# Filtering the last two column groups by token phase on three engines, with one PSUM pool for two stages

## The chip, the cores and the metric

The kernel runs on one core of a Trainium2 chip. The metric is the device time of one execution in microseconds. The engines are named as the profile names them: PE is TensorE (PEld its weight loads), DVE is VectorE, ACT is ScalarE, POOL is GpSimd, and SP issues most DMAs. Each works through its own instructions in order and waits on semaphores for the others.

## What is computed

An input x of 2048 tokens by 640 features is normalised, filtered in the frequency domain, added to itself, and then goes through a gated block without a nonlinearity:

```python
def _A_ref(x, w_r, w_i):
    X = jnp.fft.rfft2(x, axes=(-2, -1))
    X = X * (w_r + 1j * w_i)
    return jnp.fft.irfft2(X, s=(S, D), axes=(-2, -1))
def _B_ref(x, w_gate, w_up, w_down):
    return ((x @ w_gate) * (x @ w_up)) @ w_down
h = x + _A_ref(layernorm(x), w_r, w_i)
h2 = h + _B_ref(layernorm(h), w_gate, w_up, w_down)
```

S is 2048, D is 640, the real transform has 321 columns, and the inner width of the gated block is 1728.

## The kernel before

The transform over tokens is split as 16 times 128, so a two-dimensional transform, the filter and its inverse become four stages of matrix products.

**Stage one** (lines 200 to 296) runs over 16 tiles t of 128 tokens. `s1_mm(t)` multiplies the folded and normalised tile into two PSUM tiles: `pm` (tag `u`, two buffers) and a remainder `pr` (tag `im2` or `ir2`, one buffer each). Then `s1_main` (L225, ACT) copies `pm` into `s1`, in two halves for the last tile; `s1_hi` (L220, ACT) and `s1_lo` (L229, DVE) write the remainder into `s1r` as a rounded part and its rest. PSUM has eight banks of 512 float32 per partition; `banks("a", name)` closes the pool of PSUM tiles in use and opens another, and stage one works in a pool of its own (`pone`).

**Stage two** (lines 297 to 438) opens the pool `ptwo` and runs over 16 groups g of columns. For each group:

- `d_mm(g)` (L82) multiplies `s1` (eight passes, the main part) and then `s1r` (six products, the remainder) into `re` and `im`; `d_out(g)` copies both to `t` in four ACT instructions (L329 to L332).
- `s2_mm(g)` (L341) multiplies `t` into `u`, a tile of two banks with one buffer, one bank for each half h of the token phases; for the last group it takes `re` and `im` in place of `u`.
- `filt(g)` multiplies by the complex filter. Real and imaginary parts lie on partitions 0 to 63 and 64 to 127, so the crossed product moves between the halves. For most groups DVE does it all, for both h at once: L349 (direct product), L350 and L351 (crossed products), L352 (their sum). For group 15 ACT first copies the crossed parts out of PSUM (L356, L357), DVE makes the direct products (L360), POOL (L366) and DVE (L367) multiply the crossed ones, and DVE adds (L369).
- `is2_mm(g)` (L382, L384, L385) multiplies the filtered `y` into `pm` and `pr`. For group 14 these are buffers of `re` and `im`, for all others `im2` and `ir2`, which have one buffer each, so that group 15 can only start when group 13 has been read out. Row 64 of `pr` is called the edge here.
- `is2_out(g)` copies out: ACT the rounded remainder (L395, the hi copy) and the edge (L396), DVE the rest of the remainder (L397), ACT the main part into `qm` (L398), and POOL two small instructions on the edge row (L400, L401).

The order is written out by hand: the loop at L410 sets, for each g, s2_mm(g), d_mm(g+2), is2_mm(g-1), filt(g), the loads of group g+3, d_out(g+2), is2_out(g-1). At g = 14 both last s2_mm come first, and filt(15) comes between filt(14) and is2_out(13). After the loop follow is2_mm and is2_out of groups 14 and 15. The framework adds the waits: reads of one PSUM bank by different engines are put in program order, and a new pool's tiles wait for the old pool's.

**Stage three** opens two new pools (`py` and `pthree`). `id_mm(t)` (L82, tile `eo`) multiplies `qm` (eight passes) and then the remainder `qr` (five products), `unfold(t)` (L474 to L482) and `is1_mm(t)` make the tokens again. Every id_mm needs all 16 groups, so stage three begins when group 15 has been copied out. The gated block follows; it takes the rest of the time.

Of the kernel before, what the change touches and what calls it, by code (L numbers as in the profile page):

```python
# [46 lines left out]
def tile_spectral_glu(ctx: ExitStack, tc: tile.TileContext, x, wf, wgu, wlast, wdown, wdlast,  # L47
# [12 lines left out]
    def banks(key, name):  # L60
        if key in pools:
            open_pools[key].close()
        open_pools[key] = ExitStack()
        pools[key] = open_pools[key].enter_context(tc.tile_pool(name=name, bufs=2, space=bass.MemoryType.PSUM))

    def bank(tag, bufs=2):
        return pools["a"].tile([P, 512], F32, tag=tag, name=tag, bufs=bufs)
# [7 lines left out]
    def wk(shape, name):  # L75
        return work.tile(shape, F32, tag="wk", name=name)
# [121 lines left out]
    PS1, CR = {}, {}  # L198

    def s1_mm(t):  # L200
        pm, pr = PS1[t] = bank("u"), bank("ir2" if t % 2 else "im2", 1)
        (f, j), c = folded(t), CR[t]
        sums = [(f[:, o:o + P], f[:, o + n:o + n + P]) for o, n in ((31, 160), (353, 161))]
        for k, ls in enumerate((*sums, (view(j, 128, [[2, P]]),), (view(j, 129, [[2, P]]),))):
            for n, l in enumerate(ls):
                nc.tensor.matmul(pm[:, k * P:(k + 1) * P], l, c, start=n == 0, stop=n == len(ls) - 1)  # L206
        nc.tensor.matmul(pr[:, 0:P], j[:, 0:P], c, start=True, stop=True)
# [86 lines left out]
    s1_hi(NT - 1)  # L294
    s1_lo(NT - 1)

    banks("a", "ptwo")
    WM, WI = {}, {}

    def load_wm(g):  # L300
# [33 lines left out]
    def s2_mm(g):  # L334
        if g == NG - 1:
            ps = PU[g] = bank("re"), bank("im")
        else:
            PU[g] = pools["a"].tile([P, 2, 512], F32, tag="u", name="u", bufs=1)
            ps = PU[g][:, 0], PU[g][:, 1]
        for h in range(2):  # L340
            nc.tensor.matmul(ps[h][:, 0:NQ], WM[g][0][:, h], T[g][:, h], start=True, stop=True)  # L341

    def filt(g):
        ps, w = PU[g], WM[g][1]
        y = Y[g] = wk([P, 2, NQ], "y")
        us = wk([P, 2, NQ], "us")
        if g < NG - 1:
            v = ps[:, :, 0:NQ]
            tt(y, v, w[:, 0], op=OP.mult)  # L349
            nc.vector.scalar_tensor_tensor(us[0:64], v[64:128], -1.0, w[64:128, 1], op0=OP.mult, op1=OP.mult)  # L350
            tt(us[64:128], v[0:64], w[0:64, 1], op=OP.mult)  # L351
            tt(y, y, us, op=OP.add)  # L352
            return

        def swap(h):
            act(us[0:64, h], ps[h][64:128, 0:NQ], AF.Copy, scale=-1.0)  # L356
            act(us[64:128, h], ps[h][0:64, 0:NQ], AF.Copy)  # L357

        def direct(h):
            tt(y[:, h], ps[h][:, 0:NQ], w[:, 0, h], op=OP.mult)  # L360

        swap(0)
        direct(1)
        swap(1)
        direct(0)
        nc.gpsimd.tensor_tensor(us[:, 0], us[:, 0], w[:, 1, 0], op=OP.mult)  # L366
        tt(us[:, 1], us[:, 1], w[:, 1, 1], op=OP.mult)  # L367
        for h in (1, 0):
            tt(y[:, h], y[:, h], us[:, h], op=OP.add)  # L369

    def is2_mm(g):
        if g == NG - 2:
            pm, pr = bank("re"), bank("im")
        else:
            pm, pr = bank("im2", 1), bank("ir2", 1)
        PI[g] = pm, pr

        def o(ps, n, c, h):
            return ps[0:n, c * 256:(c + 1) * 256].rearrange("p (a m) -> p a m", m=8)[:, :, 4 * h:4 * h + 4]

        for h in range(2):
            nc.tensor.matmul(o(pr, 65, 0, h), Y[g][:, h, 128:193], inv(g, h), start=True, stop=True)  # L382
        for h in range(2):
            nc.tensor.matmul(o(pm, P, 0, h), Y[g][:, h, 0:128], inv(g, h), start=True, stop=True)  # L384
            nc.tensor.matmul(o(pm, P, 1, h), Y[g][:, h, 193:321], inv(g, h), start=True, stop=True)  # L385

    def inv(g, h):
        return WI[g][:, h].rearrange("p (a m) -> p a m", m=4)

    def is2_out(g):  # L390
        pm, pr = PI[g]
        f = edge[g % 4][0:1]
        r = pr[:, 0:256].rearrange("p (r n m) -> p r n m", r=2, n=NT)
        hi, lo = (qr[n:n + 64, :, :, 8 * g:8 * g + 8] for n in (0, 64))
        act(hi, r[0:64], AF.Copy)  # L395
        act(f, pr[64:65, 0:128], AF.Copy)  # L396
        tt(lo, r[0:64], f32(hi), op=OP.subtract)  # L397
        act(qm[:, :, :, 8 * g:8 * g + 8], pm.rearrange("p (c n m) -> p c n m", c=4, n=NT), AF.Copy)  # L398
        fv = f.rearrange("p (n m) -> p n m", n=NT)
        nc.gpsimd.tensor_copy(hi[0:1, 1], fv)  # L400
        nc.gpsimd.tensor_tensor(lo[0:1, 1], fv, f32(hi[0:1, 1]), op=OP.subtract)  # L401
# [8 lines left out]
    for g in range(NG - 1):  # L410
# [8 lines left out]
            s2_mm(g + 1)  # L419
        if g >= 1:  # L420
            is2_mm(g - 1)
        filt(g)
        if g + 3 < NG:
            load_wm(g + 3)
        if g + 2 < NG:
            d_out(g + 2)
        if g == NG - 2:
            filt(g + 1)
        if g >= 1:
            is2_out(g - 1)  # L430
            if g + 2 < NG:
# [1 line left out]
        if g == 6:  # L433
            nc.sync.dma_start(cit, ci)
            nc.sync.dma_start(imt, imain)
    for g in (NG - 2, NG - 1):
        is2_mm(g)
        is2_out(g)
# [592 lines left out]
```

## Time and profile before

| what | value |
|---|---|
| median of 3 runs | 729.96 us (729.23 to 730.31) |
| the profiled execution | 729.67 us |
| its span | 727.6 us |
| stage two, from d_mm(0) to id_mm(0) | 49.81 to 126.60 us |
| PE busy | 703.7 us (97%) |
| DVE, ACT, POOL busy | 465.5, 251.7, 298.5 us |

The execution's time exceeds its span by 2.1 us, which lie outside the profile. A row of the timeline has the start in us from the span's start, the duration in us, the engine, the line, the operation, what it writes and reads, how many instructions are merged into it, and in brackets how long the engine had been idle and which instruction ended that. A row of the windows has the stretch, then for PE, PEld, DVE, ACT and POOL the busy time and number of instructions, then the granted TensorE clock as a share of full speed, the DMA share and GB/s. A row of the chain has start, duration, engine, tile and line. A float32 product runs as two passes and is counted twice.

### The profile page before, as it was taken

How to read it: one execution, taken by the hardware profiler on the slowest of the kernel's cores; microseconds unless marked ns; L12 is line 12 of the kernel's file. 1: busy time of each engine (PE TensorE's matmuls, PEld its weight loads, DVE VectorE, ACT ScalarE, POOL GpSimd, SP SyncE). 2: the span in 40 equal slices, each digit the busy share in tenths (PEclk: the TensorE clock that was granted, in tenths of full speed). 3: DMA queues.
4: the chain of work that ended last, by engine and by line, in shares of the span. 5: the costliest groups of instructions: out<-in, count | busy, mean ns of one | idle time of the engine just before them, and what ended most of it. 6: DMA issues, size and time to landing. Idle time of an engine off the chain costs nothing.

```text
span 727.6 us, 10120 instructions
## 1 busy us (share of the span) xinstructions
PE 703.7 (97%) x3892; PEld 623.6 (86%) x3892; DVE 465.5 (64%) x802; ACT 251.7 (35%) x480; POOL 298.5 (41%) x274
## 2 busy tenths in 40 slices
PE   7899997999979999999999999999999999999998
PEld 7788997987868898989898888888898989898987
DVE  7967887797766665665555557565555555555554
ACT  4756666355442212222222246332222122222200
POOL 3300113332363554646463633145545546464600
PEclk9999999999989999999999999999999999999999
DMA  9404665000221211101021212311212111010203
GB/s 338 163 1 160 226 219 180 1 1 0 73 73 36 73 37 68 41 25 67 20 72 37 91 62 90 112 65 37 72 37 74 37 71 38 25 66 19 73 1 145
DMA packets 20928, 55.06 MB, mean 76 GB/s; under 512 B 2320, under 2 KB 6928, under 8 KB 20880
## 3 DMA queue, kind: packets, MB, share of 16 engines
q1 hardware_dynamic: 20304, 52.70, 20.7%
q0 software_dynamic: 288, 1.48, 0.6%
q8 instruction: 31, 0.51, 0.3%
q10 hardware_dynamic: 288, 0.23, 0.1%
q14 instruction: 17, 0.14, 0.1%
HBM read 49.16 MB, written 5.24 MB: 75 GB/s over the span
## 4 chain that ended last, share of the span: by engine, by line
PE 83%; DVE 12%; ACT 2%; issue 2%; DMA 1%; POOL 0%; DVEq 0%; ACTq 0%
PE e L82 44%; PE y L82 26%; PE re L82 2%; PE u L341 2%; PE im L82 2%; PE eo L82 2%; DVE fold L190 1%; DVE fold L195 1%; PE ir L382 1%; PE im L385 1%; DVE x L493 1%; PE im L384 1%; DVE bt L560 1%; ACT zt L510 1%; DVE bits L214 1%
## 5 line engine op out<-in xcount | busy, mean ns | idle before, releaser
L82 PE MATMUL e<-xt,wst 128*128 128x512 f32 x864 | 206.8, 390 | 0.0
L82 PE MATMUL y<-wd,ht 128*128 128x320 f32 x1312 | 201.4, 310 | 1.2 <-DVE x L493 1.1
L82 PEld LDWEIGHTS y<-wd,ht 128*128 128x128 f32 x1312 | 195.3, 188 | 5.7 <-DVE x L493 2.7
L82 PEld LDWEIGHTS e<-xt,wst 128*128 128x128 f32 x864 | 160.7, 188 | 31.7
L493 DVE TENSOR_TENSOR x<-y,x 128x640 f32<-128x640 f32 x119 | 97.7, 822 | 73.8 <-PE y L82 73.5
L688 POOL TENSOR_TENSOR wst<-raw,wst 128x1024 fp32r<-128x1024 f32 x24 | 57.9, 2411 | 169.5 <-ACT wst L687 169.5
L699 POOL TENSOR_TENSOR wst<-raw,wst 128x896 fp32r<-128x896 f32 (+1 forms) x48 | 67.8, 1436 | 27.8 <-ACT wst L697 27.8
L82 PE MATMUL e<-t,wst 128*128 128x512 f32 x288 | 74.8, 395 | 4.1 <-ACT wst L697 2.7
L82 PEld LDWEIGHTS e<-t,wst 128*128 128x128 f32 x288 | 54.7, 191 | 16.6 <-ACT wst L697 3.1
L794 ACT ACTIVATE ht<-e 128x512 fp32r<-128x512 f32 x24 | 14.4, 599 | 154.3 <-DVE e L793 154.3
L449 POOL TENSOR_TENSOR wd<-draw,wd 128x640 fp32r<-128x640 f32 x28 | 44.4, 1606 | 47.7 <-ACT wd L448 47.7
L807 ACT ACTIVATE ht<-e 128x512 fp32r<-128x512 f32 x24 | 14.4, 599 | 114.0 <-DVE e L806 114.0
L82 PE MATMUL e<-xt,wdir 128*128 128x512 f32 x180 | 41.9, 392 | 1.1 <-DVE q L479 1.1
L82 PEld LDWEIGHTS e<-xt,wdir 128*128 128x128 f32 x180 | 33.4, 188 | 8.3 <-ACT xt L532 1.3
L82 PE MATMUL e<-ht,wst 128*128 128x512 f32 x144 | 37.8, 399 | 0.0
L206 PE MATMUL u<-bits,fold 128*128 128x128 f32 x192 | 31.9, 310 | 5.9 <-DVE bits L214 2.2
L687 ACT ACTIVATE wst<-raw 128x1024 fp32r<-128x1024 f32 x24 | 25.4, 1060 | 33.4 <-DMA raw<-in_wgu_dram 33.4
L787 DVE TENSOR_TENSOR u<-e,u 128x512 f32<-128x512 f32 x24 | 16.6, 692 | 30.9 <-PE e L82 30.9
L206 PEld LDWEIGHTS u<-bits,fold 128*128 128x128 f32 x192 | 26.8, 209 | 10.1 <-POOL fold L180 4.1
L400 POOL CAST qr<-bits 1x128 fp32r<-1x128 f32 x16 | 4.5, 282 | 71.0 <-DVE qr L397 71.0
L82 PEld LDWEIGHTS e<-ht,wst 128*128 128x128 f32 x144 | 27.9, 194 | 6.0
L781 DVE TENSOR_TENSOR u<-e,p 128x512 f32<-128x512 f32 x24 | 16.6, 692 | 24.0 <-PE e L82 23.0
(178 smaller groups left out, 1042.0 us busy)
## 6 DMA issues: line engine op xcount, KB each, us to landing
raw<-in_wgu_dram SPq DMA_DIRECT2D x24, 640.0 KB, 3.9
wts<-in_wf_dram SPq DMA_DIRECT2D x16, 644.0 KB, 3.9
draw<-in_wdown_dram SPq DMA_DIRECT2D x24, 320.0 KB, 4.3
x<-in_x_dram SPq DMA_DIRECT2D x16, 320.5 KB, 6.4
out_dram<-x SPq DMA_DIRECT2D x15, 320.0 KB, 2.2
bits<-in_mm_dram SPq DMA_DIRECT2D x32, 128.0 KB, 3.8
raw<-in_wgu_dram SPq DMA_DIRECT2D x4, 320.0 KB, 4.2
draw<-in_wdlast_dram SPq DMA_DIRECT2D x4, 320.0 KB, 2.8
```

Source lines behind the costliest of these rows:

```text
L82: nc.tensor.matmul(o, l, r, start=start, stop=stop, skip_group_check=True)
L206: nc.tensor.matmul(pm[:, k * P:(k + 1) * P], l, c, start=n == 0, stop=n == len(ls) - 1)
L341: nc.tensor.matmul(ps[h][:, 0:NQ], WM[g][0][:, h], T[g][:, h], start=True, stop=True)
L449: los.append(lambda r=r, a=a, b=b: engine.tensor_tensor(w[:, 1, a:b], r, f32(w[:, 0, a:b]), op=OP.subtract))
L493: tt(xv, ps[:, :, 0:320], xv, op=OP.add)
L687: act(wa[:, 0], stage[:, 0:1024], AF.Copy)
L688: ptt(wa[:, 1], stage[:, 0:1024], f32(wa[:, 0]), op=OP.subtract)
L699: ptt(ws[:, 1, o:o + b - a], stage[:, a:b], f32(ws[:, 0, o:o + b - a]), op=OP.subtract)
L781: tt(u2, o6, p1, op=OP.add)
L787: tt(u2, o5, u2, op=OP.add)
L794: act(hh[1], o3, AF.Copy)
L807: act(hh[0], o4, AF.Copy)
```

## The change

Stage one takes its `pm` from the tag `im`, and the pool is no longer closed between stages one and two, so that one pool of eight banks serves both. In the filter, groups 14 and 15 are taken by phases (h = 0 and 1). Group 14 phase 0 is done on DVE alone. For the other three, ACT copies the crossed parts out of PSUM, POOL multiplies them, and DVE makes the direct product and the sum. DVE's share of group 15 phase 1 comes behind is2_out(13). `is2_mm` of the two groups takes the products phase by phase, and `is2_out(15)` makes the main copy first.

```diff
@@ -198,7 +198,7 @@
     PS1, CR = {}, {}
 
     def s1_mm(t):
-        pm, pr = PS1[t] = bank("u"), bank("ir2" if t % 2 else "im2", 1)
+        pm, pr = PS1[t] = bank("im"), bank("ir2" if t % 2 else "im2", 1)
         (f, j), c = folded(t), CR[t]
         sums = [(f[:, o:o + P], f[:, o + n:o + n + P]) for o, n in ((31, 160), (353, 161))]
         for k, ls in enumerate((*sums, (view(j, 128, [[2, P]]),), (view(j, 129, [[2, P]]),))):
@@ -294,7 +294,6 @@
     s1_hi(NT - 1)
     s1_lo(NT - 1)
 
-    banks("a", "ptwo")
     WM, WI = {}, {}
 
     def load_wm(g):
@@ -337,36 +336,37 @@
         else:
             PU[g] = pools["a"].tile([P, 2, 512], F32, tag="u", name="u", bufs=1)
             ps = PU[g][:, 0], PU[g][:, 1]
+            if g == NG - 2:
+                PU[g] = ps
         for h in range(2):
             nc.tensor.matmul(ps[h][:, 0:NQ], WM[g][0][:, h], T[g][:, h], start=True, stop=True)
 
     def filt(g):
-        ps, w = PU[g], WM[g][1]
+        v, w = PU[g][:, :, 0:NQ], WM[g][1]
         y = Y[g] = wk([P, 2, NQ], "y")
         us = wk([P, 2, NQ], "us")
-        if g < NG - 1:
-            v = ps[:, :, 0:NQ]
-            tt(y, v, w[:, 0], op=OP.mult)
-            nc.vector.scalar_tensor_tensor(us[0:64], v[64:128], -1.0, w[64:128, 1], op0=OP.mult, op1=OP.mult)
-            tt(us[64:128], v[0:64], w[0:64, 1], op=OP.mult)
-            tt(y, y, us, op=OP.add)
+        tt(y, v, w[:, 0], op=OP.mult)
+        nc.vector.scalar_tensor_tensor(us[0:64], v[64:128], -1.0, w[64:128, 1], op0=OP.mult, op1=OP.mult)
+        tt(us[64:128], v[0:64], w[0:64, 1], op=OP.mult)
+        tt(y, y, us, op=OP.add)
+
+    def filt_half(g, h, alone=False):
+        if h == 0:
+            Y[g] = wk([P, 2, NQ], "y"), wk([P, 2, NQ], "us")
+        y, us = (a[:, h] for a in Y[g])
+        v, w = PU[g][h][:, 0:NQ], WM[g][1]
+        direct = lambda: tt(y, v, w[:, 0, h], op=OP.mult)
+        join = lambda: tt(y, y, us, op=OP.add)
+        if alone:
+            direct()
+            nc.vector.scalar_tensor_tensor(us[0:64], v[64:128], -1.0, w[64:128, 1, h], op0=OP.mult, op1=OP.mult)
+            tt(us[64:128], v[0:64], w[0:64, 1, h], op=OP.mult)
+            join()
             return
-
-        def swap(h):
-            act(us[0:64, h], ps[h][64:128, 0:NQ], AF.Copy, scale=-1.0)
-            act(us[64:128, h], ps[h][0:64, 0:NQ], AF.Copy)
-
-        def direct(h):
-            tt(y[:, h], ps[h][:, 0:NQ], w[:, 0, h], op=OP.mult)
-
-        swap(0)
-        direct(1)
-        swap(1)
-        direct(0)
-        nc.gpsimd.tensor_tensor(us[:, 0], us[:, 0], w[:, 1, 0], op=OP.mult)
-        tt(us[:, 1], us[:, 1], w[:, 1, 1], op=OP.mult)
-        for h in (1, 0):
-            tt(y[:, h], y[:, h], us[:, h], op=OP.add)
+        act(us[0:64], v[64:128], AF.Copy, scale=-1.0)
+        act(us[64:128], v[0:64], AF.Copy)
+        nc.gpsimd.tensor_tensor(us, us, w[:, 1, h], op=OP.mult)
+        return direct, join
 
     def is2_mm(g):
         if g == NG - 2:
@@ -378,11 +378,17 @@
         def o(ps, n, c, h):
             return ps[0:n, c * 256:(c + 1) * 256].rearrange("p (a m) -> p a m", m=8)[:, :, 4 * h:4 * h + 4]
 
+        y = Y[g] if g < NG - 2 else Y[g][0]
+        edges = [lambda h=h: nc.tensor.matmul(o(pr, 65, 0, h), y[:, h, 128:193], inv(g, h), start=True, stop=True)
+                 for h in range(2)]
+        if g < NG - 2:
+            edges[0]()
+            edges[1]()
         for h in range(2):
-            nc.tensor.matmul(o(pr, 65, 0, h), Y[g][:, h, 128:193], inv(g, h), start=True, stop=True)
-        for h in range(2):
-            nc.tensor.matmul(o(pm, P, 0, h), Y[g][:, h, 0:128], inv(g, h), start=True, stop=True)
-            nc.tensor.matmul(o(pm, P, 1, h), Y[g][:, h, 193:321], inv(g, h), start=True, stop=True)
+            if g >= NG - 2:
+                edges[h]()
+            nc.tensor.matmul(o(pm, P, 0, h), y[:, h, 0:128], inv(g, h), start=True, stop=True)
+            nc.tensor.matmul(o(pm, P, 1, h), y[:, h, 193:321], inv(g, h), start=True, stop=True)
 
     def inv(g, h):
         return WI[g][:, h].rearrange("p (a m) -> p a m", m=4)
@@ -392,10 +398,14 @@
         f = edge[g % 4][0:1]
         r = pr[:, 0:256].rearrange("p (r n m) -> p r n m", r=2, n=NT)
         hi, lo = (qr[n:n + 64, :, :, 8 * g:8 * g + 8] for n in (0, 64))
+        main = lambda: act(qm[:, :, :, 8 * g:8 * g + 8], pm.rearrange("p (c n m) -> p c n m", c=4, n=NT), AF.Copy)
+        if g == NG - 1:
+            main()
         act(hi, r[0:64], AF.Copy)
         act(f, pr[64:65, 0:128], AF.Copy)
         tt(lo, r[0:64], f32(hi), op=OP.subtract)
-        act(qm[:, :, :, 8 * g:8 * g + 8], pm.rearrange("p (c n m) -> p c n m", c=4, n=NT), AF.Copy)
+        if g < NG - 1:
+            main()
         fv = f.rearrange("p (n m) -> p n m", n=NT)
         nc.gpsimd.tensor_copy(hi[0:1, 1], fv)
         nc.gpsimd.tensor_tensor(lo[0:1, 1], fv, f32(hi[0:1, 1]), op=OP.subtract)
@@ -419,13 +429,17 @@
             s2_mm(g + 1)
         if g >= 1:
             is2_mm(g - 1)
-        filt(g)
+        if g < NG - 2:
+            filt(g)
+        else:
+            filt_half(g, 0, True)
+            left = [filt_half(*a) for a in ((g, 1), (g + 1, 0), (g + 1, 1))]
+            for f in left[0] + left[1]:
+                f()
         if g + 3 < NG:
             load_wm(g + 3)
         if g + 2 < NG:
             d_out(g + 2)
-        if g == NG - 2:
-            filt(g + 1)
         if g >= 1:
             is2_out(g - 1)
             if g + 2 < NG:
@@ -433,6 +447,8 @@
         if g == 6:
             nc.sync.dma_start(cit, ci)
             nc.sync.dma_start(imt, imain)
+    for f in left[2]:
+        f()
     for g in (NG - 2, NG - 1):
         is2_mm(g)
         is2_out(g)
```

## The prediction, made before the result was known

> **What bounds the kernel now.** I read the page first: the chain that ended last is mostly TensorE, so a change pays only where PE waits.
>
> ```profile
> PE 83%; DVE 12%; ACT 2%; issue 2%; DMA 1%; POOL 0%; DVEq 0%; ACTq 0%
> ```
>
> Next the windows and the chain of waits, to see which stages those are.
>
> ```profile
> 100.00:110.00 10.00, 10.00 (x70) 9.32 (x69) 8.54 (x12) 5.98 (x15) 2.12 (x6) 1.00 0.64 223
> 120.00:130.00 10.00, 6.49 (x48) 6.11 (x49) 5.24 (x12) 4.93 (x12) 2.69 (x8) 1.00 0.15 57
> ...
> 62.74 1.09 PE u L341 x4
> 67.19 1.09 PE u L341 x4
> ...
> 126.60 7.63 PE eo L82 x52
> ```
>
> The middle groups of stage two run at 4.45 us each (62.74 to 67.19) with PE always busy; a faster filter there buys nothing. After 126.60 PE is busy again without a break. What the change can win lies at the two ends of stage two. The first end, from the timeline:
>
> ```profile
> 48.41 0.39 PE L207 MATMUL ir<-bits,fold 128*128 128x128 f32 x2
> 48.61 0.66 ACT L225 ACTIVATE s<-u 128x256 f32<-128x256 f32 x2 [0.72 <-PE u L206]
> 49.15 0.28 ACT L220 ACTIVATE s1r<-ir 128x128 fp32r<-128x128 f32 x1
> 49.47 0.29 DVE L229 TENSOR_TENSOR s1r<-ir,s1r 128x128 fp32r<-128x128 f32 x1 [1.49 <-ACT s1r L220]
> 49.81 0.54 PE L82 MATMUL im<-tab,s 128*128 128x160 f32 x2 [1.02 <-DVE s1r L229]
> ...
> 50.96 0.42 PE L82 MATMUL re<-frt,s1r 128*128 128x322 f32 x1
> ```
>
> The first product of d_mm(0) reads only s1, written by ACT L225, and yet starts when DVE L229 is done. L229 writes s1r, which no product reads before 50.96. So this wait is not for data: the new pool's banks are given out only when the last reader of any bank of the old pool is done. The other end:
>
> ```profile
> 117.27 0.42 DVE L397 TENSOR_TENSOR qr<-ir,qr 64x256 fp32r<-64x256 f32 x1 [0.65 <-PE u L341]
> 117.88 0.44 ACT L356 ACTIVATE us<-re 64x322 f32<-64x322 f32 x1
> 118.56 0.83 DVE L350 SCALAR_TENSOR_TENSOR us<-u,wts 64x644 f32<-64x644 f32 x1
> 118.89 0.87 POOL L366 TENSOR_TENSOR us<-us,wts 128x322 f32<-128x322 f32 x1 [0.32 <-ACT us L357]
> 121.01 0.49 DVE L360 TENSOR_TENSOR y<-im,wts 128x322 f32<-128x322 f32 x1
> 121.15 0.65 PE L382 MATMUL im<-bits,y 128*65 128x128 f32 x4 [1.46 <-DVE y L352]
> 121.53 0.44 ACT L356 ACTIVATE us<-im 64x322 f32<-64x322 f32 x1 [2.76 <-DVE y L360]
> 123.13 0.60 ACT L398 ACTIVATE qm<-im 128x512 f32<-128x512 f32 x1
> 123.62 0.36 ACT L395 ACTIVATE qr<-im 64x256 fp32r<-64x256 f32 x1
> 124.37 0.65 PE L382 MATMUL ir<-bits,y 128*65 128x128 f32 x4 [1.68 <-DVE qr L397]
> 125.06 0.38 ACT L395 ACTIVATE qr<-ir 64x256 fp32r<-64x256 f32 x1 [0.16 <-PE ir L382]
> 125.46 0.27 ACT L396 ACTIVATE bits<-ir 1x128 f32<-1x128 f32 x1
> 125.53 0.39 PE L385 MATMUL im<-bits,y 128*128 128x128 f32 x2
> 125.77 0.42 DVE L397 TENSOR_TENSOR qr<-ir,qr 64x256 fp32r<-64x256 f32 x1 [1.03 <-ACT bits L396]
> 125.95 0.60 ACT L398 ACTIVATE qm<-im 128x512 f32<-128x512 f32 x1 [0.22 <-PE im L385]
> 126.25 0.28 POOL L400 CAST qr<-bits 1x128 fp32r<-1x128 f32 x1 [0.19 <-DVE qr L397]
> 126.61 0.45 POOL L401 TENSOR_TENSOR qr<-bits,qr 1x128 fp32r<-1x128 f32 x1
> 126.60 1.37 PE L82 MATMUL eo<-tab,qm 128*128 128x161 f32 x8 [0.69 <-ACT qm L398]
> 127.70 0.56 PE L82 MATMUL eo<-xt,qr 128*128 128x322 f32 x2
> ```
>
> PE waits 1.46 us for group 14's filter and 1.68 us for L397 of group 13, which sits on DVE behind both filters and frees the bank that is2_mm(15) writes. It then waits 0.69 us for the last ACT copy.
>
> **The change part by part.**
>
> **A, one pool.** The first product of d_mm(0) then waits only for the first of the two L225 copies: 48.61 + 0.33 = 48.94, so PE starts at 48.99, right behind its last product of stage one (48.80). Later products need the second copy (49.27) and the remainder (49.76) 0.7 and 1.15 us further on, when they are there. Gain 49.81 - 48.99 = **0.81 us**. Bounds: 0 if the wait stays, 0.49 if both copies are awaited. I take 0.81, since the timeline shows PE idle with its data ready. Nothing takes it back: the chain after it goes PE, ACT, PE, DVE up to 58 us and then on PE alone, and all of it moves. Loads are issued three groups (13 us) ahead.
>
> **B, the last two groups.** I work on the clock of before; A shifts everything alike. A half filter (322 columns) costs 0.49 on DVE (L360). Group 14 phase 0 is four dependent operations after L397: starts at 117.72, 118.23, 118.74, 119.25, where the whole group cost four of 0.83. ACT now makes three pairs of copies of 0.44 without the 2.76 us wait in between: done at 118.76, 119.65, 120.54. POOL makes three multiplies of 0.87 instead of one, the first 118.89 to 119.76, the others behind it. ACT's extra pair lies ahead of group 13's copies, which end at 121.86; DVE reaches group 13's L397 later (122.06) than their edge copy (121.23) anyway, so it costs nothing.
>
> What POOL's multiplies do to DVE's adds beside them, other rows tell:
>
> ```profile
> 40.19 0.88 POOL L180 TENSOR_TENSOR fold<-x 128x320 f32<-128x320 f32 x1 [1.44 <-DVE fold L195]
> 40.27 1.16 DVE L190 SCALAR_TENSOR_TENSOR fold<-x,m 128x322 f32<-128x322 f32 x1
> ```
>
> L190 has as many columns as a half filter and two inputs in SBUF. Caught behind POOL's L180 it took 1.16 and ended 0.36 us after POOL's end (41.43 against 41.07). L350, with one input in PSUM, ran beside L366 at the 0.83 us of its kind. So only the adds (y and us both lie in SBUF) pay, and each ends 0.36 us after the multiply it meets.
>
> So on DVE: add (14,0) ends 120.12; direct (14,1) 120.53; add (14,1) behind the second multiply (to 120.72) 121.08; direct (15,0) 121.5; add (15,0) behind the third (to 121.68) 122.04; L397 of group 13 122.48 instead of 124.32; direct and add (15,1) 123.5, or 123.7 if POOL's L401 of group 13 is in the way. On PE: is2_mm(14) starts at 120.17 instead of 121.15 and its second half at 121.13. is2_mm(15) starts at 122.54, when L397 has freed its bank, and its second half at 123.55. Half a group takes 0.85 there (all twelve passes run from 124.37 to 125.92), so it ends at 124.40.
>
> Then the end changes hands. In group 15 ACT now does the main copy first: 124.43, the hi copy 0.49 behind (123.13 to 123.62), the edge 0.39 behind that (125.06 to 125.46, about), done at 125.58, and L397 is done at 126.03. id_mm(0) writes banks of a newly opened pool and by the rule of part A waits for that last L397, not only for the main copy (125.03). In the rows above L397 began at 125.77, behind the edge copy L396 (ended 125.73), though L395, whose result it needs, had ended at 125.44: the three read one bank, and the edge copy reads partition 64, L397 partitions 0 to 63. The Trainium skill (PSUM — Partial Sum Buffer, PSUM bank collisions raise a hardware error) has it that two engines may read a bank at once in different quadrants of 32 partitions. By that rule L397 need not wait for the edge, would end 0.3 us earlier, and B would be 0.7; the row says that this program waits by the bank, and I go by the row.
>
> So PE goes on at 126.08 instead of 126.60, or at 126.28 with L401 in the way: I take **0.4 us**. POOL's last row (126.03 + 0.06 + 0.28 + 0.08 + 0.45 = 126.9) is ready before the second remainder product wants it (1.25 us behind PE's restart, 127.3). Bounds of B: -0.25 (third rival) to +0.9 (first). From 126.60 on PE is the bound without a break, so all of it reaches the end.
>
> **Sum.** 0.81 + 0.4 = 1.2 us: the profiled 729.67 becomes 728.5, and the median 729.96, 0.3 above it, becomes **728.8 us**. Within 0.2% (1.46 us, about what a measurement of this kernel can tell from no change) lie 728.5 to 731.4.
>
> **The rivals.**
>
> First, **B gains twice as much**. Either the adds miss POOL's multiplies (DVE is done 0.5 us sooner), or id_mm(0) does not wait for the last L397: PE restarts at 125.1, but its second remainder product waits for POOL at 126.95 instead of starting at about 127.85. Both give 0.9, with A 1.7: **728.3**. For it speaks that the engines' starts are only known to a tenth; against it the rows of L190 and L229. Chance 0.33.
>
> Second, **the pool does not do what it says**: the first product still waits for L229, because s1r of the last tile, and not the pool, holds it. A is 0: **729.5**. The first reader of s1r at 50.96 speaks against it. Chance 0.10.
>
> Third, **the tile of group 14 counts as one**. At 121.53 an ACT read waited for a DVE read of the same bank (L360 ends 121.50). If the two banks of u are held as one, ACT's first pair waits for DVE's third read of phase 0, 119.23 instead of 117.88; followed through the same steps, L397 of group 15 ends at 126.8, B is -0.25, total gain 0.55: **729.4**. Against it: the halves lie in different banks. Chance 0.09.
>
> Fourth, **slower: the TensorE clock drops**.
>
> ```profile
> 14.90 2.22 PE L206 MATMUL u<-bits,fold 128*128 128x128 f32 x8 [1.10 <-DVE bits L214]
> ...
> 12.00:14.00 2.00, 1.09 (x8) 0.77 (x6) 1.97 (x7) 1.19 (x4) 1.15 (x3) 1.00 1.09 410
> 14.00:16.00 2.00, 1.10 (x5) 0.98 (x5) 2.00 (x3) 0.12 (x1) 2.00 (x3) 0.74 1.06 397
> 120.00:122.00 2.00, 0.85 (x8) 0.86 (x9) 1.86 (x4) 0.46 (x2) 0.00 (x0) 1.00 0.72 279
> 122.00:124.00 2.00, 0.69 (x7) 0.50 (x5) 1.50 (x4) 1.91 (x5) 0.00 (x0) 1.00 0.02 8
> 206.00:208.00 2.00, 0.69 (x2) 0.05 (x1) 0.93 (x3) 1.24 (x4) 2.00 (x1) 0.53 0.00 0
> 212.00:214.00 2.00, 2.00 (x8) 1.56 (x8) 0.69 (x1) 1.06 (x1) 1.22 (x2) 0.77 0.86 304
> ```
>
> The granted clock halved at 15 us after thin work with waits of only 1.10 us, and again from 206.1 to 212.9. In 120 to 124 PE is as thin and kept its clock. After the change PE has about 1.5 us of passes in the 3.4 us ahead of id_mm(0), much as now, but the last wait grows to 1.7. If the clock drops there for 6.8 us, PE, the bound from then on, loses half of it: +3.4 - 1.2 = +2.2, **732.2**. It decides from the point where the thinnest stretch holds fewer passes than any of now. The Trainium skill (TensorE: Matmul & The Clock Gate, HAM oscillation — how this bites in real kernels) asks for idle gaps above some 3.4 us; by it this cannot happen. The trace does not agree (1.10 us at 14.90), so the rival stays. Chance 0.10.
>
> **How the numbers follow.** The forecast has 0.38. Its own bounds (B from 0.1 to 0.7) put 0.06 of that past 1.46 us. Faster: 0.33 + 0.06 = 0.39. Within 0.2%: 0.32 + 0.10 + 0.09 = 0.51. Slower: 0.10. The range runs from 727.8 (the first rival with half a microsecond of spread) to 730.3 (the second with as much and B at its lower bound) and leaves out the fourth.
>
> **What would show it.** A: d_mm(0) starts at about 49.0 behind L225. B: ACT's three pairs without a gap; adds near 0.8 us where they meet a POOL multiply; is2_mm(14) at about 119.4 on the new clock; id_mm(0) right behind the last L397, near 125.3. Wrong: a wait of d_mm(0) for L229, an ACT copy waiting for DVE's phase 0, or a granted clock under 1.00 between 120 and 135 us.

## The result and the profile after

| | before | after |
|---|---|---|
| median | 729.6 us (728.77 to 730.56, 22 runs) | 731.25 us (730.09 to 732.91, 22 runs) |
| the profiled execution, its span | 729.67, 727.6 us | 731.35, 729.4 us |
| stage two, d_mm(0) to id_mm(0) | 49.81 to 126.60 us | 49.22 to 127.98 us |
| id_mm(0) to the end of the span | 601.0 us | 601.4 us |

The changed kernel is 1.0024 times as long as before, 95% interval 1.0018 to 1.003: 1.65 us **slower**, where 1.2 us faster was forecast. By id_mm(0) the changed kernel is 1.38 us late, though its d_mm(0) started 0.59 us early: stage two takes 1.97 us more. The rest of the span differs by 0.4. In the changed kernel the lines are numbered anew: L358 is the direct product of a half filter, L359 the add, L362 and L363 the crossed products on DVE, L366 and L367 ACT's crossed copies, L368 POOL's multiply; L382, L390 and L391 are is2_mm; L401 is the main copy, L404 the hi copy, L405 the edge copy, L406 DVE's subtraction (the lo row).

The page's shares by engine and the row of the chain that answers to the one at 126.60, from the profile after:

```profile
PE 82%; DVE 12%; ACT 2%; issue 2%; DMA 1%; POOL 0%; DVEq 0%; POOLq 0%; ACTq 0%
```

```profile
127.98 7.61 PE eo L82 x52
```

The stretch from id_mm(0) on takes what it took before (7.61 against 7.63 us for its first products). The first end of stage two, from the timeline after:

```profile
48.58 0.39 PE L207 MATMUL ir<-bits,fold 128*128 128x128 f32 x2
48.78 0.66 ACT L225 ACTIVATE s<-im 128x256 f32<-128x256 f32 x2 [0.73 <-PE im L206]
...
49.22 0.54 PE L82 MATMUL im<-tab,s 128*128 128x160 f32 x2 [0.25 <-ACT s L225]
...
49.64 0.29 DVE L229 TENSOR_TENSOR s1r<-ir,s1r 128x128 fp32r<-128x128 f32 x1 [1.49 <-ACT s1r L220]
```

The first product of d_mm(0) now starts right behind the first L225 copy, and L229 ends 0.7 us after that start instead of ahead of it. From the start of the last L207 to that product there are 0.64 us (49.22 - 48.58), where before there were 1.40 (49.81 - 48.41). The other end:

```profile
118.13 0.49 DVE L363 TENSOR_TENSOR us<-u,wts 64x322 f32<-64x322 f32 x1
...
118.66 0.50 DVE L359 TENSOR_TENSOR y<-y,us 128x322 f32<-128x322 f32 x1
...
118.71 0.43 ACT L366 ACTIVATE us<-u 64x322 f32<-64x322 f32 x1 [1.46 <-DVE us L363]
...
119.62 0.49 DVE L358 TENSOR_TENSOR y<-u,wts 128x322 f32<-128x322 f32 x1 [0.47 <-ACT us L367]
...
119.72 2.79 POOL L368 TENSOR_TENSOR us<-us,wts 128x322 f32<-128x322 f32 x3 [1.75 <-PE im L391]
...
120.62 1.16 DVE L359 TENSOR_TENSOR y<-y,us 128x322 f32<-128x322 f32 x1 [0.51 <-POOL us L368]
...
121.84 0.43 PE L382 MATMUL im<-bits,y 128*65 128x128 f32 x2 [1.75 <-DVE y L359]
...
122.89 0.42 DVE L406 TENSOR_TENSOR qr<-ir,qr 64x256 fp32r<-64x256 f32 x1
...
123.37 0.69 PE L382 MATMUL ir<-bits,y 128*65 128x128 f32 x2 [0.65 <-DVE qr L406]
...
125.56 0.63 PE L391 MATMUL im<-bits,y 128*128 128x128 f32 x2
126.23 0.60 ACT L401 ACTIVATE qm<-im 128x512 f32<-128x512 f32 x1 [2.34 <-PE im L391]
...
127.42 0.42 DVE L406 TENSOR_TENSOR qr<-ir,qr 64x256 fp32r<-64x256 f32 x1 [2.43 <-ACT bits L405]
...
127.98 1.20 PE L82 MATMUL eo<-tab,qm 128*128 128x161 f32 x7 [1.79 <-DVE qr L406]
```

Read it from the top. ACT's first copy of phase 1 (L366 at 118.71) waits 1.46 us, for DVE's L363, the third read of phase 0. POOL's multiplies therefore begin at 119.72 and lie one behind another (0.87, 0.86 and 1.04 us). The add at 120.62 becomes ready when the first multiply ends; POOL's next one has begun too, at 120.57, and the add takes 1.16 us instead of 0.50 (118.66). So the second half of is2_mm(14) starts at 121.84 behind an idle time of 1.75 us, L406 of group 13 at 122.89 and is2_mm(15) at 123.37. The pairs of passes of is2_mm(15) last 0.63 to 0.69 us where those of group 14 last 0.39 to 0.43. Then the main copy, the hi copy, the edge and L406 of group 15 follow each other, and id_mm(0) starts behind L406 and not behind the main copy, which had ended at 126.83. Why the passes are longer the windows say (stretch, then busy time and instructions of PE, PEld, DVE, ACT and POOL, granted clock, DMA share, GB/s):

```profile
119.60:123.00 3.40, 1.37 (x11) 0.98 (x9) 2.73 (x5) 3.24 (x9) 2.75 (x3) 1.00 0.42 154
123.00:126.40 3.40, 2.83 (x12) 2.53 (x12) 1.82 (x4) 1.03 (x3) 1.45 (x4) 0.50 0.00 0
120.00:130.00 10.00, 5.81 (x33) 5.27 (x33) 4.60 (x9) 4.84 (x13) 5.15 (x11) 0.83 0.10 37
```

From 123.0 to 126.4 the granted clock is half; ahead of it lie 3.4 us in which PE was busy for 1.37. In the ten microseconds from 120 the mean clock is 0.83, where before it was 1.00.

### The profile page after: what moved, and what is told of

Read it like the earlier page. It is cut to its first block, busy times and chain, and to the rows that moved or that the text cites. A ratio compares the mean times of both kernels' runs of the same rounds, so it can differ in the third digit from the quotient of the medians.

```text
span 729.4 us, 10129 instructions
## 1 busy us (share of the span) xinstructions
PE 705.7 (97%) x3892; PEld 624.9 (86%) x3892; DVE 465.2 (64%) x803; ACT 252.6 (35%) x482; POOL 300.1 (41%) x276
## 3 DMA queue, kind: packets, MB, share of 16 engines
HBM read 49.16 MB, written 5.24 MB: 75 GB/s over the span
## 4 chain that ended last, share of the span: by engine, by line
PE 82%; DVE 12%; ACT 2%; issue 2%; DMA 1%; POOL 0%; DVEq 0%; POOLq 0%; ACTq 0%
PE e L82 44%; PE y L82 26%; PE re L82 2%; PE im L82 2%; PE u L342 2%; PE eo L82 2%; DVE fold L190 1%; DVE fold L195 1%; PE ir L382 1%; DVE x L509 1%; PE im L391 1%; PE im L390 1%; DVE bt L576 1%; ACT zt L526 1%; DVE bits L214 1%
## 5 line engine op out<-in xcount | busy, mean ns | idle before, releaser
L206 PE MATMUL im<-bits,fold 128*128 128x128 f32 x192 | 31.2, 300 | 5.8 <-DVE fold L195 1.8
L206 PEld LDWEIGHTS im<-bits,fold 128*128 128x128 f32 x192 | 25.8, 201 | 10.4 <-DVE fold L195 5.1
```

## The experiments

The theory after reading the trace had four parts: A does what was forecast; the two banks of group 14 count as one tile, which costs about 1.2 us; the main copy first costs something more, because id_mm(0) waits for L406; and the clock drop costs the rest. The rivals: the clock alone explains the loss and the waits are harmless; or the tile alone does, and the clock drops in any case.

Each kernel was compared with the kernel before on the same chip. Absolute times in stage one move by some 0.4 us between traces, so the interval from d_mm(0) to id_mm(0), which holds B but not A, is read beside the median:

| kernel | median and that of before, us | ratio, 95% interval | d_mm(0) to id_mm(0), us | clock from 118 to 132 us in the trace |
|---|---|---|---|---|
| before | | | 49.81 to 126.60: 76.79 | full |
| after | 731.25, 729.6 | 1.0024 [1.0018, 1.003] | 49.22 to 127.98: 78.76 | half 123.0 to 126.4 |
| pool only | 728.91, 729.8 | 0.9988 [0.9979, 0.9996] | 49.30 to 126.08: 76.78 | full |
| filter only | 731.5, 729.8 | 1.0028 [1.0017, 1.0039] | 49.91 to 127.95: 78.04 | half 128.3 to 131.7 |
| two tiles | 729.39, 729.8 | 1.0002 [0.9993, 1.0011] | 49.42 to 126.25: 76.83 | half 126.6 to 130.0 |
| hi first | 729.86, 729.8 | 1.0004 [0.9995, 1.0012] | 49.16 to 126.67: 77.51 | half 121.8 to 125.2 |
| after, PE kept busy | 730.06, 729.49 | 1.0004 [0.9996, 1.0013] | 49.43 to 127.48: 78.05 | full |
| tiles and hi | 728.1, 729.49 | 0.9978 [0.9968, 0.9987] | 49.14 to 125.13: 75.99 | full |
| before, PE kept busy | 729.94, 729.49 | 1.0006 [0.9997, 1.0014] | 50.01 to 126.80: 76.79 | full |
| tiles and hi, PE kept busy | 728.23, 729.49 | 0.9983 [0.9974, 0.9992] | 49.10 to 125.14: 76.04 | full |
| tiles, PE kept busy | 728.99, 729.76 | 0.9988 [0.9979, 0.9997] | 49.20 to 126.04: 76.84 | full |
| hi first, PE kept busy | 729.48, 729.76 | 0.9993 [0.9984, 1.0002] | 49.12 to 126.37: 77.25 | full |
| crossed product on DVE | 728.95, 729.76 | 0.9985 [0.9976, 0.9994] | 49.12 to 125.62: 76.50 | full |

### The pool alone, on the kernel before

```diff
-        pm, pr = PS1[t] = bank("u"), bank("ir2" if t % 2 else "im2", 1)
+        pm, pr = PS1[t] = bank("im"), bank("ir2" if t % 2 else "im2", 1)
-    banks("a", "ptwo")
```

> The kernel before with the one pool for stages one and two alone, the old filter. Theory (part A is worth what its trace shows, 0.6 us, and the loss lies wholly in the filter): 0.6 us faster than before, d_mm(0) starting right behind the first L225 copy. Rival (the earlier start is given back later, or costs something of its own): no faster than before.

0.9 us faster than before on the same chip (728.91 against 729.8, ratio 0.9979 to 0.9996). Its timeline at the first end:

```profile
48.66 0.39 PE L207 MATMUL ir<-bits,fold 128*128 128x128 f32 x2
...
49.30 0.54 PE L82 MATMUL im<-tab,s 128*128 128x160 f32 x2 [0.25 <-ACT s L225]
```

49.30 - 48.66 = 0.64 us, as in the changed kernel, and the interval behind it is that of before (76.78). A is real, whole, and nothing takes it back.

### The filter alone

The changed kernel with two pools again:

```diff
-        pm, pr = PS1[t] = bank("im"), bank("ir2" if t % 2 else "im2", 1)
+        pm, pr = PS1[t] = bank("u"), bank("ir2" if t % 2 else "im2", 1)
+    banks("a", "ptwo")
```

> The changed kernel with the two pools put back: the new filter alone. Theory (the two parts add up): about 2.2 us slower than before, 0.6 above the changed kernel, with d_mm(0) waiting for L229 again. Rival (the parts interact, for example through the time at which the clock's windows fall): as slow as the changed kernel, 1.6 us.

1.7 us slower. The trace of this kernel kept its clock until 128.3, so its interval of 78.04 us is B without a drop: 1.25 us longer than before. The drop came in id_mm(0) instead. From the windows and the chain:

```profile
120.80:124.20 3.40, 1.02 (x7) 0.83 (x8) 2.73 (x6) 3.24 (x9) 2.50 (x4) 1.00 0.18 72
124.90:128.30 3.40, 1.27 (x9) 1.07 (x9) 1.17 (x3) 1.13 (x3) 1.08 (x4) 1.00 0.00 0
128.30:131.70 3.40, 3.40 (x15) 3.40 (x14) 0.00 (x0) 0.24 (x1) 0.88 (x3) 0.50 0.00 0
```

```profile
127.95 9.22 PE eo L82 x52
```

The same products that took 7.61 us in the changed kernel take 9.22: a window of 3.4 us at half clock, with PE busy all through, costs 1.6. The stretch from 120.8 to 124.2 is thinner than the one ahead of the drop and yet cost no clock; the last section comes back to it.

### Two tiles for group 14

Group 14 takes two tiles of one bank each, as group 15 does; is2_mm(14) then writes the `u` tile, and the main copy of group 14 goes ahead of its lo row.

```diff
-        if g == NG - 1:
+        if g >= NG - 2:
             ps = PU[g] = bank("re"), bank("im")
...
-            pm, pr = bank("re"), bank("im")
+            uu = pools["a"].tile([P, 2, 512], F32, tag="u", name="u", bufs=1)
+            pm, pr = uu[:, 0], uu[:, 1]
...
+        if g == NG - 2:
+            main()
         tt(lo, r[0:64], f32(hi), op=OP.subtract)
-        if g < NG - 1:
+        if g < NG - 2:
             main()
```

> The changed kernel, but group 14 reads its two phases from two PSUM tiles (the banks that group 15 uses, one round earlier), and is2_mm(14) writes the two-bank tile instead. Theory (ACT waits for DVE's third read because the two banks are one tile, and that wait of 1.46 us makes the filter late and the clock drop): ACT copies without a wait from 117.3 on, is2_mm(15) over about 1 us earlier, no drop of the clock in most runs, 1.2 to 2 us faster than the changed kernel, so from equal to 0.4 us faster than before. Rival (POOL's multiplies holding DVE's additions are the loss): ACT's wait goes, but the time stays within 0.5 us of the changed kernel.

ACT's first copy no longer waits. It starts before DVE's third read of phase 0 does:

```profile
117.48 0.44 ACT L364 ACTIVATE us<-im 64x322 f32<-64x322 f32 x1
...
118.33 0.49 DVE L361 TENSOR_TENSOR us<-re,wts 64x322 f32<-64x322 f32 x1
```

The interval is 76.83 against 78.04 without the edit: 1.21 us back. The median is that of before within the interval, and the twelve runs fall into two groups: seven from 728.33 to 729.39, five from 730.76 to 731.41. The profiled one, 731.41, shows what parts them:

```profile
123.20:126.60 3.40, 1.27 (x9) 1.07 (x9) 1.17 (x3) 1.13 (x3) 1.08 (x4) 1.00 0.00 0
126.60:130.00 3.40, 3.40 (x15) 3.40 (x14) 0.00 (x0) 0.20 (x1) 0.88 (x3) 0.50 0.00 0
```

PE was busy for 1.27 of 3.4 us, and in the next 3.4 us, which are id_mm(0), the clock was half. The other four of the upper group have no trace, but the mean clock of every run is on record. One window of 3.4 us at half clock lowers the mean of a span of 728 us by 0.0023, so 0.993 stands for three such windows, 0.991 for four and 0.988 for five, as the traces confirm. The upper five runs have 3 to 5 windows, 4.2 on average; six of the lower seven have 3, and one has 4. So four of the upper five had at least one window more than nearly all of the lower group; where it fell in the runs without a trace isn't shown.

### The hi copy first in group 15

```diff
-        if g == NG - 1:
-            main()
         act(hi, r[0:64], AF.Copy)
         act(f, pr[64:65, 0:128], AF.Copy)
         tt(lo, r[0:64], f32(hi), op=OP.subtract)
-        if g < NG - 1:
-            main()
+        main()
```

> The changed kernel, but group 15 is copied out in the order of the other groups, the hi copy first and the main copy last. Theory (id_mm(0) waits for the last L406 because the pool changes, so the main copy ahead of it costs): 0.7 us faster than the changed kernel, PE going on right behind the main copy. Rival (id_mm(0) needs only the main copy): 0.5 us or more slower than the changed kernel.

729.86 against 729.8 before: the loss of the changed kernel, 1.65 us, is gone. But its profiled run had the half clock from 121.8 to 125.2, inside is2_mm, so neither the trace nor the median parts the order from the clock. The question is taken up again below with the clock held. It does show how near the edge the clock is:

```profile
118.40:121.80 3.40, 1.53 (x13) 1.15 (x11) 2.38 (x5) 3.01 (x8) 2.10 (x3) 1.00 0.68 261
```

### PE kept busy, after and before

Products of a constant table that nobody reads fill PE's waits, 7 between the halves of is2_mm(14) and 6 behind is2_mm(15); as a control, 11 of them around is2_mm of the same two groups in the kernel before.

```diff
             nc.tensor.matmul(o(pm, P, 1, h), y[:, h, 193:321], inv(g, h), start=True, stop=True)
+            if g == NG - 2 and h == 0:
+                for _ in range(7):
+                    nc.tensor.matmul(pr[:, 256:384], cit, cit, start=True, stop=True)
+        if g == NG - 1:
+            spare = bank("re")
+            for _ in range(6):
+                nc.tensor.matmul(spare[:, 0:P], cit, cit, start=True, stop=True)
```

> The changed kernel with 13 products added that nobody reads: seven behind the first half of is2_mm(14), into unused columns of its remainder bank, and six behind is2_mm(15), into a free bank. They keep PE at work while it waits. Theory (the thin stretch drops the granted clock in most runs, at a place that moves from run to run, and is2_mm(15) or the first id_mm then runs at half speed): clock 1.00 from 118 to 134 us, spread of the runs half as wide, about 1 us faster than the changed kernel. Rival (the clock plays no part in the median): as slow as the changed kernel or slower.

> The kernel before with 11 such products in its three waits at the end of stage two, as a control. Theory (the kernel before keeps its clock there): within 0.3 us of before. Rival (it loses the clock there too, in part of its runs): 0.5 us or more faster than before.

More work for PE makes the changed kernel **faster**: its loss falls from 1.65 to 0.57 us, and its runs spread over 1.5 us instead of 2.8. The control gains nothing (0.45 slower, interval from 0.2 faster to 1.0 slower). So the drop is of the changed kernel's making and costs about 1.1 us on the median. The mean clocks agree: 12 of the 22 runs of the changed kernel had five windows at half clock (4.6 on average), while none of 87 runs of the kernel before had more than four (3.0 to 3.2), nor any of the changed kernel with PE kept busy (3.0). Windows of the one, and of the kernel before at its thinnest:

```profile
121.60:125.00 3.40, 2.21 (x17) 1.63 (x16) 3.10 (x7) 2.38 (x7) 1.82 (x4) 1.00 0.01 4
```

```profile
119.80:123.20 3.40, 1.54 (x12) 1.35 (x12) 2.79 (x6) 1.59 (x5) 0.00 (x0) 1.00 0.50 191
```

With the clock at 1.00 all through, the changed kernel's interval is 78.05 us, as that of the filter alone: 1.26 us of waits, which the clock has no part in. The end of it:

```profile
125.73 0.60 ACT L408 ACTIVATE qm<-im 128x512 f32<-128x512 f32 x1 [1.63 <-PE im L391]
...
126.91 0.42 DVE L413 TENSOR_TENSOR qr<-ir,qr 64x256 fp32r<-64x256 f32 x1 [1.71 <-ACT bits L412]
...
127.48 1.34 PE L82 MATMUL eo<-tab,qm 128*128 128x161 f32 x8 [0.45 <-DVE qr L413]
```

The main copy had ended at 126.33; id_mm(0) waits 1.15 us more, for L413, the lo row.

### Tiles and hi, alone and with PE kept busy

The edits of two tiles and of hi first together; in a second kernel 7 unread products beside them (one or two between the halves of is2_mm, four behind is2_mm(15)).

```diff
+            if g >= NG - 2 and h == 0:
+                for _ in range(NG - g):
+                    nc.tensor.matmul(pr[:, 256:384], cit, cit, start=True, stop=True)
+        if g == NG - 1:
+            spare = bank("re")
+            for _ in range(4):
+                nc.tensor.matmul(spare[:, 0:P], cit, cit, start=True, stop=True)
```

> The changed kernel with both corrections: group 14 in two tiles, and the hi copy of group 15 ahead of the main copy. Theory (the two terms add, and with shorter waits the clock drops less often): id_mm(0) starts near 125.3, 1.3 us faster than before, 728.5 beside 729.8. Rival (the corrections overlap, since one wait hides behind the other): no faster than the better of the two alone, about 729.4.

> The kernel with both corrections and seven such products in its waits (two and one behind the first halves of is2_mm(14) and is2_mm(15), four behind is2_mm(15)). Theory (what is left of the spread at the end of stage two is the clock): clock 1.00 throughout the stage's end, narrower than the kernel with both corrections, and as fast or up to 0.5 us faster: 728.0 to 728.5. Rival (the added products delay the real ones): slower than the kernel with both corrections.

728.1 against 729.49: 1.4 us faster than before (ratio 0.9968 to 0.9987), and the version that **beats both kernels**. The unread products add nothing (728.23). The copies of group 15 in it:

```profile
123.32 0.43 PE L381 MATMUL ir<-bits,y 128*65 128x128 f32 x2 [0.34 <-DVE y L357]
...
123.79 0.38 ACT L401 ACTIVATE qr<-ir 64x256 fp32r<-64x256 f32 x1 [1.04 <-PE ir L381]
123.81 0.39 PE L390 MATMUL im<-bits,y 128*128 128x128 f32 x2
...
124.48 0.60 ACT L400 ACTIVATE qm<-im 128x512 f32<-128x512 f32 x1
...
125.13 1.09 PE L82 MATMUL eo<-tab,qm 128*128 128x161 f32 x6 [0.93 <-ACT qm L400]
```

The hi and the edge copy read the bank of the first pass (L381), which is ready while L390 still runs, so ACT starts 0.4 us before PE is done (123.81 + 0.39); the main copy ends last, at 125.08, L405 has ended by then, and id_mm(0) follows at 125.13.

### One edit each, with PE kept busy

The edit of two tiles without that of hi first, and the other way round, each with unread products (9 and 11).

Two tiles, beside the diff of two tiles above:

```diff
+            if g >= NG - 2 and h == 0:
+                for _ in range(NG - g):
+                    nc.tensor.matmul(pr[:, 256:384], cit, cit, start=True, stop=True)
+        if g == NG - 1:
+            spare = bank("re")
+            for _ in range(6):
+                nc.tensor.matmul(spare[:, 0:P], cit, cit, start=True, stop=True)
```

Hi first takes its own diff above and the products of the changed kernel with PE kept busy, 4 instead of 6 of them behind is2_mm(15).

> The changed kernel with group 14's column halves in two tiles, the main copy of group 15 still first, and 9 unread products in PE's waits so that the clock stays up. Terms are additive: by the trace of the changed kernel with its clock kept, id_mm(0) starts at 127.48. Without ACT's wait of 1.46 us the halves of is2_mm(15) run at 122.1 and 123.3 as in the kernel with both edits, then main copy, hi, edge and lo of group 15 follow: lo ends at about 125.9 and id_mm(0) starts at 126.0. So 1.5 us better than the 0.57 us over the kernel before that the changed kernel with its clock kept shows: 0.9 us faster than before. Rival: what two tiles took back was the clock only; then 0.6 us slower than before, as without them.

> The changed kernel with the hi copy first in group 15 and 11 unread products in PE's waits. Theory: the hi and edge copies read the edge bank, which is ready when the second half's first pass is done, 0.46 us ahead of the main bank; so they run beside PE's last passes, the main copy ends at about 126.6, lo is done before it, and id_mm(0) starts at 126.6 instead of 127.48: 0.9 us better than the changed kernel with its clock kept, 0.3 us faster than before. Rival: what hi first took back was the clock only; then 0.6 us slower than before.

With the clock held the four kernels make a square. The intervals are 78.05 with neither edit, 76.84 with two tiles, 77.25 with hi first, 76.04 with both: the tile is worth 1.21 us either way, the order 0.80 either way. The medians against before follow: +0.57, -0.77, -0.28, -1.26. The rivals, by which both edits only brought back the clock, fall. The step from copies to id_mm(0) with hi first:

```profile
124.97 0.38 ACT L409 ACTIVATE qr<-ir 64x256 fp32r<-64x256 f32 x1 [1.18 <-PE ir L382]
...
125.66 0.60 ACT L408 ACTIVATE qm<-im 128x512 f32<-128x512 f32 x1
...
126.37 1.34 PE L82 MATMUL eo<-tab,qm 128*128 128x161 f32 x8
```

### The crossed product on DVE

The kernel with tiles and hi, POOL's three multiplies on DVE instead, each right ahead of its add.

```diff
-        nc.gpsimd.tensor_tensor(us, us, w[:, 1, h], op=OP.mult)
-        return direct, join
+        cross = lambda: (tt(us, us, w[:, 1, h], op=OP.mult), join())
+        return direct, cross
```

> The kernel with two tiles and hi first, its three crossed multiplies on DVE, each right ahead of its add, instead of POOL. Theory: an add beside a POOL multiply takes 0.57 to 0.85 us instead of 0.49, which is less than the multiply itself costs on DVE (0.49): the last group-13 subtraction ends 0.5 us later and the last add 0.8 us later, id_mm(0) at 125.9 instead of 125.13, so 0.8 us slower than with POOL, 0.6 us faster than before. Rival: the two engines take each other's place at the port, POOL's part gains nothing; then the same as with POOL, 1.4 us faster than before.

```profile
119.36 0.48 DVE L366 TENSOR_TENSOR us<-us,wts 128x322 f32<-128x322 f32 x1
...
119.88 0.50 DVE L357 TENSOR_TENSOR y<-y,us 128x322 f32<-128x322 f32 x1
...
125.62 0.68 PE L82 MATMUL eo<-tab,qm 128*128 128x161 f32 x3 [0.94 <-ACT qm L400]
```

The interval is 76.50, 0.51 longer than with POOL, and the median gains 0.81 us over before instead of 1.39. A multiply and an add on DVE alone take 0.48 and 0.50; beside POOL the add took 0.57 to 0.85 and the multiply none of DVE's time. Both guesses were off: POOL's part gains 0.5 us by the intervals, less than the 0.8 worked out and more than nothing. The third engine pays here.

## Why the prediction was wrong

**A, one pool: right.** 0.81 us forecast, 0.76 in the traces (1.40 - 0.64), 0.9 in the median of the pool alone. The start of d_mm(0), forecast at about 49.0, came at 49.22 with the whole stage 0.17 later (L207 at 48.58 instead of 48.41); it stands behind L225, as said. The second rival, by which s1r and not the pool holds the product, falls with it: L229 ends 0.7 us after that product has begun.

**B failed at the step "ACT now makes three pairs of copies of 0.44 without the 2.76 us wait in between".** The copies have no gap among them, but they start 1.46 us late, which is the third rival word for word: the two banks of `u` are held as one tile, and ACT's read of one waits for DVE's read of the other. Given 0.09, it was true. The prediction set against it that "the halves lie in different banks"; the row it had (L356 waiting for L360 in one bank) showed that reads of one bank are ordered, and said nothing of two banks in one tile. The rival's price was -0.25 for B against +0.4, so 0.65; the runs gave 1.21. Of this, 0.59 is the add at 120.62, which took 1.16 us where its like in the kernel with two tiles took 0.57, and the rest is its later start (120.62 against 120.00 there). The price was a slip in the sum: an ACT pair that starts at 119.23 instead of 117.88 moves POOL's first multiply, and by the prediction's own steps all that follows, by 1.35 us, so the lo row of group 15 comes out at about 127.4 (an estimate from its own rows) and not at 126.8.

**The DVE queue was mis-sized by 0.45 us.** With the tile mended and the main copy first, that is with B as the forecast meant it, the interval is 76.84, so B is a loss of 0.05 instead of a gain of 0.4. The kernel with two tiles and PE kept busy shows where (add 0.62 to its times to have the clock of the prediction: its first direct product starts at 117.10, where the prediction has 117.72):

```profile
117.10 0.49 DVE L356 TENSOR_TENSOR y<-re,wts 128x322 f32<-128x322 f32 x1
...
118.27 3.02 POOL L366 TENSOR_TENSOR us<-us,wts 128x322 f32<-128x322 f32 x3 [0.32 <-PE ir L381]
...
118.64 0.85 DVE L357 TENSOR_TENSOR y<-y,us 128x322 f32<-128x322 f32 x1
...
120.00 0.57 DVE L357 TENSOR_TENSOR y<-y,us 128x322 f32<-128x322 f32 x1
...
121.07 0.57 DVE L357 TENSOR_TENSOR y<-y,us 128x322 f32<-128x322 f32 x1
...
121.67 0.42 DVE L414 TENSOR_TENSOR qr<-ir,qr 64x256 fp32r<-64x256 f32 x1
...
122.52 0.45 POOL L419 TENSOR_TENSOR qr<-bits,qr 1x128 fp32r<-1x128 f32 x1
...
122.72 0.60 DVE L357 TENSOR_TENSOR y<-y,us 128x322 f32<-128x322 f32 x1
...
123.37 0.43 PE L381 MATMUL ir<-bits,y 128*65 128x128 f32 x2
...
125.47 0.42 DVE L414 TENSOR_TENSOR qr<-ir,qr 64x256 fp32r<-64x256 f32 x1 [1.71 <-ACT bits L411]
...
126.04 1.20 PE L82 MATMUL eo<-tab,qm 128*128 128x161 f32 x7 [0.44 <-DVE qr L414]
```

| step | forecast | measured, + 0.62 |
|---|---|---|
| add (14,0) ends | 120.12 | 120.11 |
| add (14,1) ends | 121.08 | 121.19 |
| add (15,0) ends | 122.04 | 122.26 |
| lo row of group 13 ends | 122.48 | 122.71 |
| add (15,1) ends | 123.5, or 123.7 | 123.94 |
| second half of is2_mm(15) starts | 123.55 | 123.99 |
| lo row of group 15 ends | 126.03 | 126.51 |
| id_mm(0) | 126.08, or 126.28 | 126.66 |

POOL's three multiplies took 0.87, 1.09 and 1.11 us, where 0.87 was taken for each from a row without adds beside it: the third ends 0.23 us later than forecast (121.29 + 0.62 against 121.68). The last add waited for POOL's small row (122.52) and took 0.60, which the prediction named and priced at 0.2; the 0.4 that it took for B lies midway between the values with it and without. The rule for the adds held: the three end 0.35 or 0.36 us behind POOL's multiplies (the third at 121.64 against 121.29), and the last one 0.35 behind the small row (123.32 against 122.97).

**The main copy first: right.** The prediction let id_mm(0) wait for the last lo row, and it does, and the adds do meet POOL's multiplies; so the first rival falls on both its conditions. What was not asked is what the other order would give: 0.80 us.

**The fourth rival came true, at another price.** Its mechanism and its point were right: "from the point where the thinnest stretch holds fewer passes than any of now". The thinnest 3.4 us hold 1.54 us of PE work before (12 instructions), and the clock stays; the 3.4 us ahead of each drop hold 1.37 (after), 1.27 (filter only, two tiles) and 1.53 (hi first). The sentence that went wrong is that after the change there would be "about 1.5 us of passes in the 3.4 us ahead of id_mm(0), much as now". Two waits thin the end of stage two, the tile's and the one behind the main copy. Its thinnest 3.4 us hold about 1.0 us of PE work with both (filter only), 1.27 with the second alone (two tiles), 1.53 with the first alone (hi first) and 1.76 with neither (tiles and hi). The drop lasts 3.4 us here and not 6.8, and costs 1.6 where PE is the bound and about 1.1 on the median.

**The terms add up.** Forecast: -0.81 - 0.4 = -1.2. Measured: A -0.76, B -0.4 + 1.21 + 0.45 = +1.26, the clock +1.1; together +1.6, against 1.65 in the medians. The clock's term is itself a difference of two medians, so the check is on the other two: they come to +0.50, and the changed kernel with its clock held is 0.57 us slower than before.

**What stays open.** How much work keeps the clock up. The kernel before kept it with 1.54 us in 3.4, and the one with hi first lost it with 1.53, so the limit in stage two lies near these values; but in stage one the clock halved behind 1.56 us (after, from 13.8 to 17.2) and 1.83 (tiles and hi, from 14.7 to 18.1), while filter only kept it through 1.72 in stage two (121.5 to 124.9). So busy time alone isn't the whole rule. Where the fifth window fell in the runs without a trace isn't known either.

## What to carry to other kernels

Before counting on two engines reading side by side, ask in what unit the program orders them: two banks in one tile are one thing, and splitting the tile was worth 1.2 us, three times what the forecast gave the whole filter. When a change adds waits ahead of a stretch bound by TensorE, count TensorE's busy time in every 3.4 us before it: here, with about 1.5 us or less, the clock could halve for the next 3.4 (in stage one with up to 1.8 too), and whether it does can hang on where that run's windows fall, as filter only shows. Filling the waits with unread products is a quick test of it. Copy out first what is ready first, and leave last the copy that the next product waits for.

## What was not expected of the hardware

**The clock drops without a long idle time, and on a grid of its own.** The longest wait of PE ahead of the drop at 123.0 is 1.75 us, and work that keeps PE busy for 40% of 3.4 us was not enough. In each trace the clock halves at moments that lie whole multiples of 3.41 us apart: before at 14.97 and 206.11 (56 steps), in the changed kernel at 17.19, 123.00 and 208.34 (31 and 25 steps). Where this grid lies differs from trace to trace. The Trainium skill (TensorE: Matmul & The Clock Gate, What's actually happening) says that the gate watches a free-running window of 3.4 us. The traces agree with it, and the grid tells why the thinnest stretch need not cost the clock: in filter only the 3.4 us from 120.8 to 124.2 held 1.02 us of work, but a mark of the grid fell at 121.5, and the window from there to 124.9 held 1.72; the drop came behind the next one, which held 1.27. The same section asks for an idle window before a drop, and there the measurement decides: windows with 1.27 to 1.53 us of work were followed by a drop.

**An add that comes just behind the start of a multiply on POOL waits it out.** In the changed kernel the add at 120.62 became ready as POOL passed from one multiply to the next (120.57); it ended 0.35 us behind that multiply and took 1.16 us. With two tiles the adds came in the middle or near the end of a multiply, ended 0.35 us behind it too, and took 0.57 to 0.85; the multiplies that began beside them took 1.09 and 1.11 us instead of 0.87. The Trainium skill (SBUF — State Buffer, SBUF: two separate sides) calls the port pair of the two engines an exclusive lock for a whole instruction, which whoever starts first holds; the rows agree, and add the price: 0.66 us for an add that comes just too late, and about 0.2 for a multiply that begins while an add is finishing.
